# Down projection and attention output of a fused block as row-tiled units of 64 rows

## The chip, the cores and the metric

The kernel runs on one core of a Trainium2 chip. The metric is the device time of one execution in microseconds (us). Five engines run side by side, each through a queue of its own: TensorE (PE in the profile; its weight loads are listed apart as PEld), VectorE (DVE), ScalarE (ACT), GpSimd (POOL) and SyncE (SP), which here only starts DMAs. TensorE writes its sums to PSUM, which the kernel uses as eight banks of 128 partitions by 512 float32 numbers (the tile `ps_all`). ScalarE and VectorE read them from there.

## The reference

```python
x  = A_x                                  # (1, 2048, 576), bfloat16
xn = layernorm(x)
qkv = xn @ A_wqkv                         # 32 heads of 18
pq, pk = phi(q), phi(k)                   # phi(t) = (t + 1 if t > 0 else exp(t)) + 1e-6
kv, z = einsum(pk, v), sum(pk)            # per head: 18 x 18, and 18
o  = (pq @ kv) / (pq . z + 1e-6)
attention = o @ A_wo                      # 576 x 576
ffn = (gelu(xn @ B_w_gate) * (xn @ B_w_up)) @ B_w_down      # 576 -> 4608 -> 576
out = x + attention + ffn
```

## The kernel before, in words

**Tokens and stages.** The 2048 tokens are 16 tiles of 128 (`NS`); four tiles make a stage of 512 tokens (`sc`, `NSC` = 4, `TPC` = 4). The head of the kernel (until about 75.8 us) normalises x, transposes it into `xnT`, projects K for all tokens and Q for the first stage, runs the first 14 gate/up tiles (`RAW`), and builds the 32 products kv of all tokens as blocks on the diagonal of `kvT`. `kvT` holds five chunks of heads: four of 7 heads (126 rows) and one of 4 heads (72 rows).

**A stage.** The loop over `sc` (L955) does for each stage, in this order: the Q projection of the stage's four tiles (`late_q`, L855, from the second stage on; stage 0 has its Q from the head), gate/up (`gu_pair`, L804, 18 calls of two units each, of which stage 0 has the last 11), and the down part (L968 to 989). `hT` then holds gelu(gate) * up of the stage, 36 slices of 128 (`NF`).

**Two forms of matmul.** Gate/up and the Q projection contract over 576 = 4 x 128 + 64. They are built as `_Unit` (L242): the array is used as two row tiles, rows 0 to 63 (`LO`) and 64 to 127 (`HI`), which work side by side on different banks. In the first part (`p1`), LO adds to the unit's first bank and HI to its second, step by step. In the second part (`p2`) they change banks: LO adds to the second bank and HI to the first. In between, an empty instruction on GpSimd (`swap`, L263) waits for the last matmul of the first part, and the second part's first matmul on the second bank waits for it. The order in `gu_pair` and `late_q` puts another unit's part between the two parts of a unit. All these matmuls are issued at L253. The down part uses the whole array, 128 rows to one bank.

**The down part before.** A tile (`_DownTile`, L905) takes two banks, one for each half of the 576 output columns (288 and 288; the very last tile 448 and 128, `LAST_MID`). `down` (L929) issues for one half the 36 matmuls over `hT` and w_down (L935) and the 4 over the first four chunks of the attention (L940: `pqT`, the normalised and transposed Q features, against `m_sb`, the product kv x Wo). The fifth chunk has 64 rows and is kept twice, in LO and in HI; `pair` (L921) runs it for both halves side by side, as two half-array matmuls (L923). Tiles 0 and 1 of a stage run `pair` first; tiles 2 and 3 run it after all of the stage's `down` calls, or, in the last stage, before tile 2's. `add` (L945) lets VectorE add x to one half (L949); SyncE writes the tile out.

**kv x Wo.** `m_sb` is made once, in stage 0. The fifth chunk is made by `m_last_unit` (L880), a `_Unit` of one step in gate/up block `M_UNIT` = 10; ScalarE copies it to `m_last`, and SyncE's DMAs spread it in blocks 12 and 14. The other four are made by `m_product` (L870): two full-array matmuls each (L875) put between the down matmuls of tile 0's first half, at f = 8, 14, 20 and 26, with a copy by ScalarE after each.

**What sets the order.** From L704 on the program's order is the order of the instructions on each engine; nothing reorders them. Banks are handed out in pairs by a ring (`two_banks`, L126): four pairs, so a pair comes back after four grants, and its next user waits for its last reader. `load_late_wq` (L865) refills `wo2` with the Q weights once its Wo has been used. All weight loads and outputs stand in one queue, SyncE's.

```python
def p2(self):
    for kt in self.then:
        m = self.mm(1, LO, kt, False, kt == self.then[-1])
        if kt == self.then[0]:
            tc.add_manual_dep(m.ins, self.turn.ins.name, SYNC, ...)
        self.mm(0, HI, kt, False, kt == self.then[-1])
```

Of the kernel before, what the change touches and what calls it, by code (L numbers as in the profile page):

```python
# [14 lines left out]
P = 128  # L15
HP = 64
# [3 lines left out]
DH = 18  # L20
F = 4608
NS = S // P
NF = F // P
SC = 512
NSC = S // SC
TPC = SC // P
HALF = D // 2
KT = 5
HCH = [7, 7, 7, 7, 4]
HOFF = [0, 7, 14, 21, 28]  # L30
NCH = len(HCH)
# [58 lines left out]
def kernel(  # L90
# [11 lines left out]
    nc = tc.nc  # L102
# [14 lines left out]
    ps_all = psum.tile([P, 8, 512], F32, name="ps_all")  # L117
# [4 lines left out]
    LO, HI = slice(0, HP), slice(HP, P)  # L122
# [3 lines left out]
    def two_banks(ring=banks):  # L126
        return [ring.next(), ring.next()]
# [3 lines left out]
    kvT = persist.tile([P, NCH, CR], BF16, name="kvT")  # L131
# [8 lines left out]
    hT = h_store[:].rearrange("p (f t) -> p f t", t=SC)  # L140
# [137 lines left out]
    def gu_unit(blk, i, two, relay):  # L278
        wg, wu = gu_blocks[blk]
        wr = wr_pairs[blk // 2]  # L280
        c0 = (blk % 2) * GUB * P + i * P
        at = blk // NB * SC

        def lhs(a, rows, kt):
            if kt == 4:
                return wr[rows, c0:c0 + P]
            return (wg, wu)[a][rows, kt, i * P:(i + 1) * P]

        return _Unit(
            [ps_all[:, b, :] for b in two], lhs, lambda a, rows, kt: xnT[rows, kt, at:at + SC], relay,  # L290
        )
# [92 lines left out]
    for n in range(NS):  # L384
        first = 1.5 * n if n < 4 else 9.0 + 3.0 * (n - 4)
# [154 lines left out]
    for name in line:  # L540
# [3 lines left out]
        kind, n = name[0], int(name[1:].rstrip("ab"))  # L544
# [4 lines left out]
        if kind == "t":  # L549
            two = (tp_banks[n], tp_banks[n] + 1)  # L550
# [6 lines left out]
        if name[-1] == "b":  # L557
            u = pending[-1 if name[:2] == pending[-1].name else -2]
# [3 lines left out]
        u = _Chain()  # L562
        u.name, u.at = name[:2] if name[-1] == "a" else name, clock
        if kind in "KQ":
            u.body = _Token(kind, n, head_banks if u.name in HEAD_T else banks)
            b = u.body.banks
# [6 lines left out]
        else:  # L573
            u.body = _Raw(n)
            b = u.body.two
            blk = n // GUB
# [103 lines left out]
    def z_stage(two):  # L680
# [12 lines left out]
        out=bm3, in_=bm3, compare_op=ALU.is_ge, fill=0.0, base=0, pattern=[[-DH, 7], [0, DH]], channel_multiplier=1,  # L693
    )
    nc.gpsimd.affine_select(
        out=bm3, in_=bm3, compare_op=ALU.is_ge, fill=0.0, base=DH - 1, pattern=[[DH, 7], [0, DH]], channel_multiplier=-1,
# [40 lines left out]
    wo2 = late_pool.tile([P, NCH, D], BF16, name="wo2")  # L737
    m_sb = late_pool.tile([P, NCH, D], BF16, name="m_sb")
    m_last = late_pool.tile([P, D], BF16, name="m_last")
    pqT = late_pool.tile([P, NCH, S], BF16, name="pqT")  # L740
# [5 lines left out]
    def wd(f):  # L746
        return wd_a[:, f, :] if f < WD_A else wd_m[:, f - WD_A, :] if f < WD_B else wd_c[:, f - WD_B, :]

    def load_wo():
        nc.sync.dma_start(wo2[:CR, 0:4, :], A_wo[0:4 * CR, :].rearrange("(c p) j -> p c j", p=CR))  # L750
        nc.sync.dma_start(wo2[:D - 4 * CR, 4, :], A_wo[4 * CR:D, :])
# [46 lines left out]
    for n in range(NS):  # L798
        late = n % TPC > 0
        den_jobs += [(den_mul, n)] + late * [(den_transpose, n - 1)] + [(den_inv, n), (den_scale, n)]  # L800
        den_jobs += (n % TPC == TPC - 1) * [(den_transpose, n)]
    M_UNIT, M_TAILS, M_ROWS = RAW // GUB + 3, RAW // GUB + 5, RAW // GUB + 7

    def gu_pair(sc, k):  # L804
        blk = sc * NB + k
        units = []
        aside = m_last_unit() if blk == M_UNIT else None
        if aside:
            aside.p1()
        for i in range(GUB):  # L810
            b = two_banks()
            u = gu_unit(blk, i, b, nc.gpsimd)
            if blk > RAW // GUB:
                load_gu(blk + NWBUF - 1, i)
            u.p1()
            units.append((b, u))
        if sc == 0 and k == RAW // GUB:
            load_wo()
        elif wd_left:
            load_wd(*wd_left.pop(0))  # L820
        if aside:
            aside.p2()
            m_last_copy(aside)
        for i, (b, u) in enumerate(units):
            u.p2()
            gl = fwork.tile([P, SC], F32, name="gl")
            nc.scalar.activation(out=gl[:], in_=ps_all[:, b[0], :], func=ACT.Gelu_apprx_tanh)  # L827
            nc.vector.tensor_tensor(out=hT[:, GUB * k + i, :], in0=ps_all[:, b[1], :], in1=gl[:], op=ALU.mult)  # L828
            for _ in range(min(len(gelus), 2)):
                gelu_now(gelus.pop(0))  # L830
            if den_jobs and ((i == 1 and 0 < k < NB - 1) if sc else 8 < k < 17):
                job, n = den_jobs.pop(0)
                job(n)
# [31 lines left out]
    def load_late_wq():  # L865
        nc.sync.dma_start(wo2[:, 0:4, :], A_wqkv[0:512, 0:D].rearrange("(kt p) c -> p kt c", p=P))
        for rows in (LO, HI):
            nc.sync.dma_start(wo2[rows, 4, :], A_wqkv[512:576, 0:D])

    def m_product(c, bank):  # L870
        rows = DH * HCH[c]
        for hf in range(2):
            b = bank(hf)
            hs = slice(hf * HALF, (hf + 1) * HALF)
            nc.tensor.matmul(  # L875
                ps_all[:rows, b, :HALF], lhsT=kvT[:rows, c, :rows], rhs=wo2[:rows, c, hs], start=True, stop=True,
            )
            nc.scalar.copy(out=m_sb[:rows, c, hs], in_=ps_all[:rows, b, :HALF])

    def m_last_unit():  # L880
        rows4 = DH * HCH[4]
        two = two_banks()
        outs = [ps_all[:rows4, b, :HALF] for b in two]
        return _Unit(
            outs, lambda i, rows, kt: kvT[rows, 4, :rows4], lambda i, rows, kt: wo2[rows, 4, i * HALF:(i + 1) * HALF],
            nc.gpsimd, first=(0,), then=(0,),
        )

    def m_last_copy(u):
        for i in range(2):  # L890
            nc.scalar.copy(out=m_last[:DH * HCH[4], i * HALF:(i + 1) * HALF], in_=u.outs[i])
# [13 lines left out]
    class _DownTile:  # L905
# [4 lines left out]

        def __init__(self, n):
            self.n, self.ts = n, slice(n * P, (n + 1) * P)
            self.banks = two_banks()
            self.opened = False
            mid = LAST_MID if n == NS - 1 else HALF
            self.parts = [slice(0, mid), slice(mid, D)]

        def acc(self, hf):
            return ps_all[:, self.banks[hf], 0:self.parts[hf].stop - self.parts[hf].start]

        def pair(self):  # L921
            for hf, rows in ((0, LO), (1, HI)):
                nc.tensor.matmul(  # L923
                    self.acc(hf), lhsT=pqT[rows, 4, self.ts], rhs=m_sb[rows, 4, self.parts[hf]],
                    start=not self.opened, stop=self.opened, skip_group_check=True,
                )
            self.opened = True

        def down(self, hf, todo):  # L929
            paired = self.opened  # L930
            j = self.n % TPC
            for f in range(NF):
                if f in todo:
                    todo[f]()
                nc.tensor.matmul(  # L935
                    self.acc(hf), lhsT=hT[:, f, j * P:(j + 1) * P], rhs=wd(f)[:, self.parts[hf]],
                    start=(f == 0 and not paired), stop=False, skip_group_check=True,
                )
            for c in range(4):
                nc.tensor.matmul(  # L940
                    self.acc(hf), lhsT=pqT[:, c, self.ts], rhs=m_sb[:, c, self.parts[hf]],
                    start=False, stop=(paired and c == 3), skip_group_check=True,
                )

        def add(self, hf):  # L945
# [9 lines left out]
    for sc in range(NSC):  # L955
        if sc:
            late_q(sc)
            nc.scalar.preload_act_table_set("gelu_apprx_tanh_and_others")
        for k in range(0 if sc else RAW // GUB, NB):
            gu_pair(sc, k)  # L960
            if sc == 0 and k in m_last_steps:
                m_last_steps[k]()
        while wd_left:
            load_wd(*wd_left.pop(0))

        if sc < NSC - 1:
            nc.scalar.preload_act_table_set("natural_log_exp_and_others")
        tiles = [_DownTile(sc * TPC + j) for j in range(TPC)]  # L968
        tiles[0].pair()
        tiles[1].pair()  # L970
        spare = tiles[2].banks + tiles[3].banks
        hooks = {8 + 6 * c: (lambda c=c: m_product(c, lambda hf: spare[(2 * c + hf) % 4])) for c in range(4)} if sc == 0 else {}
        for j, t in enumerate(tiles):
            if j == 2 and sc == NSC - 1:
                tiles[2].pair()
                tiles[3].pair()
            closed = t.opened
            for hf in range(2):
                t.down(hf, hooks if j == hf == 0 else {})
                if closed:  # L980
                    t.add(hf)
            if sc == j == 0:
                load_late_wq()
        for t in tiles[2:]:
            if sc < NSC - 1:
                t.opened = True
                t.pair()
                for hf in range(2):
                    t.add(hf)


# [28 lines left out]
```

## Time and profile before

| what | value |
|---|---|
| median of three runs | 507.29 us (507.22 to 508.05) |
| the profiled execution | 507.53 us |
| its span, first to last instruction | 505.8 us |
| TensorE's mean granted clock | 0.999 |
| matmuls and weight loads | 4768 each |

The span is divided by the stages as follows, by the starts of matmuls:

| part | start, us | length, us |
|---|---|---|
| head and kv | 0 | 75.8 |
| gate/up, stage 0 (22 units) | 75.8 | 43.0 |
| down part, stage 0 | 118.8 | 40.9 |
| late Q and gate/up, stage 1 | 159.7 | 74.3 |
| down part, stage 1 | 234.0 | 39.9 |
| late Q and gate/up, stage 2 | 273.9 | 74.3 |
| down part, stage 2 | 348.2 | 39.9 |
| late Q and gate/up, stage 3 | 388.1 | 74.3 |
| down part, stage 3 | 462.5 | 40.5 to the end of the span |

How to read it: busy time tells how long an engine had work in flight, and matmuls overlap, so one lasts longer than the distance to the next. The pace of a stream is read from the time that a piece of the chain with a known number of matmuls takes, or from the starts of two matmuls. A wait that ends on an engine other than TensorE does not lengthen the kernel while TensorE's own stream has no hole.

### The profile page before, as it was taken

The page shows a single profiled execution, that of the slowest core. Times are in us where ns is not written, and L with a number is a line of the kernel's source. Part 1 is how long each engine was busy: PE and PEld are TensorE (multiplying, and loading weights), DVE is VectorE, ACT ScalarE, POOL GpSimd, SP SyncE. Part 2 cuts the span into 40 slices and gives each one's busy share as a digit, 9 for nine tenths or more (in the row PEclk, how much of TensorE's full clock was granted, in tenths as well). Part 3 has the DMA queues.
Part 4 walks back from the last instruction along what each step waited for, and adds up shares of the span by engine and source line. Part 5 has one row for each costly group of instructions (what it writes and reads, how often), then busy time and mean ns, then how long its engine had stood idle before and what let it go on. Part 6 is the DMA issues. An engine that isn't in the chain of part 4 may idle for free.

```text
span 505.8 us, 11210 instructions
## 1 busy us (share of the span) xinstructions
PE 501.7 (99%) x4768; PEld 304.8 (60%) x4768; DVE 230.8 (46%) x483; ACT 152.0 (30%) x265; POOL 10.4 (2%) x34
## 2 busy tenths in 40 slices
PE   9999999999999999999999999999999999999997
PEld 7666784446777444446777444445777444445774
DVE  5768996773002655553002665553002665553100
ACT  6778735325001422332001522332001432232000
POOL 3110100000000000000000000000000000000000
PEclk9999999999999999999999999999999999999999
DMA  9998917993201465553001455653001455640000
GB/s 230 269 217 170 304 45 207 282 252 80 71 13 54 119 166 172 158 150 106 12 13 42 129 156 170 169 151 108 13 12 32 140 150 167 173 104 14 13 13 23
DMA packets 114123, 61.59 MB, mean 122 GB/s; under 512 B 23954, under 2 KB 114010, under 8 KB 114074
## 3 DMA queue, kind: packets, MB, share of 16 engines
q1 hardware_dynamic: 113802, 60.54, 45.3%
q8 instruction: 37, 0.61, 0.5%
q0 software_dynamic: 128, 0.21, 0.1%
q10 hardware_dynamic: 144, 0.15, 0.1%
q14 instruction: 12, 0.10, 0.1%
HBM read 53.60 MB, written 2.36 MB: 111 GB/s over the span
## 4 chain that ended last, share of the span: by engine, by line
PE 99%; DVE 0%; issue 0%
PE ps_all L253 62%; PE ps_all L935 28%; PE ps_all L636 3%; PE ps_all L940 3%; PE ps_all L231 1%; PE ps_all L923 0%; PE ps_all L644 0%; PE ps_all L663 0%; PE ps_all L358 0%; PE ps_all L875 0%; PE ps_all L237 0%; DVE res L949 0%; PE ps_all L682 0%; DVE warm L210 0%; DVE eps_ln L222 0%
## 5 line engine op out<-in xcount | busy, mean ns | idle before, releaser
L253 PE MATMUL ps_all<-xnT,wg 64*128 64x512 bf16 x1152 | 273.8, 376 | 0.0
L253 PE MATMUL ps_all<-xnT,wu 64*128 64x512 bf16 x1152 | 273.1, 376 | 0.0
L253 PEld LDWEIGHTS <-wg 64*128 64x128 bf16 x1152 | 108.3, 94 | 66.7
L253 PEld LDWEIGHTS <-wu 64*128 64x128 bf16 x1152 | 108.3, 94 | 65.4
L828 DVE TENSOR_TENSOR hT<-ps_all,gl 128x512 bf16<-128x512 f32 x130 | 89.8, 691 | 104.2 <-ACT gl L827 104.1
L935 PEld LDWEIGHTS <-hT 128*128 128x128 bf16 x1152 | 110.8, 98 | 30.9 <-issue 1.3
L827 ACT ACTIVATE gl<-ps_all 128x512 f32<-128x512 f32 x130 | 77.6, 597 | 164.1 <-PE ps_all L253 163.7
L949 DVE TENSOR_TENSOR res<-ps_all,x_sb 128x288 bf16<-128x288 f32 (+2 forms) x32 | 13.8, 455 | 146.3 <-PE ps_all L940 88.1
L935 PE MATMUL ps_all<-wd_a,hT 128*128 128x288 bf16 (+2 forms) x512 | 68.3, 286 | 0.0
L253 PE MATMUL ps_all<-xnT,wr 64*128 64x512 bf16 x288 | 54.9, 376 | 0.0
L935 PE MATMUL ps_all<-hT 128*128 128x288 bf16 (+2 forms) x384 | 52.4, 286 | 0.0
L849 ACT ACTIVATE gl<-ps_all 128x288 f32<-128x288 f32 x24 | 9.2, 409 | 121.4 <-PE ps_all L253 119.3
L935 PE MATMUL ps_all<-wd_m,hT 128*128 128x288 bf16 (+2 forms) x256 | 36.8, 286 | 0.0
L253 PEld LDWEIGHTS <-xnT 64*128 64x128 bf16 x504 | 26.6, 94 | 6.6 <-ACT xnT L363 0.3
L253 PEld LDWEIGHTS <-wr 64*128 64x128 bf16 x288 | 14.3, 94 | 16.3
L940 PE MATMUL ps_all<-m_sb,pqT 128*128 128x288 bf16 (+2 forms) x128 | 20.9, 286 | 0.0
L253 PE MATMUL ps_all<-wqkv_sb,xnT 64*128 64x288 bf16 x256 | 19.7, 283 | 0.0
L636 PE MATMUL ps_all<-hT,xn 128*128 128x288 bf16 x128 | 16.0, 286 | 0.0
L486 ACT CAST hT<-ps_all 128x1024 bf16<-128x1024 f32 x14 | 14.1, 1010 | 4.9 <-PE ps_all L253 4.5
L636 PEld LDWEIGHTS <-xn 128*128 128x128 bf16 x128 | 12.4, 98 | 3.5 <-issue 0.5
L940 PEld LDWEIGHTS <-pqT 128*128 128x128 bf16 x128 | 12.4, 98 | 3.3
L253 PE MATMUL ps_all<-wo,xnT 64*128 64x288 bf16 x216 | 13.7, 283 | 0.0
(100 smaller groups left out, 245.4 us busy)
## 6 DMA issues: line engine op xcount, KB each, us to landing
wg<-in_B_w_gate_dram SPq DMA_DIRECT2D x72, 256.0 KB, 3.0
wu<-in_B_w_up_dram SPq DMA_DIRECT2D x72, 256.0 KB, 3.5
wd_a<-in_B_w_down_dram SPq DMA_DIRECT2D x4, 576.0 KB, 8.5
wr<-in_B_w_gate_dram SPq DMA_DIRECT2D x35, 64.0 KB, 3.1
wr<-in_B_w_up_dram SPq DMA_DIRECT2D x35, 64.0 KB, 2.9
out_dram<-res SPq DMA_DIRECT2D x15, 144.0 KB, 1.8
x_sb<-in_A_x_dram SPq DMA_DIRECT2D x6, 288.0 KB, 5.0
hT<-in_B_w_down_dram SPq DMA_DIRECT2D x4, 432.0 KB, 5.6
```

Of the source, the lines that this page charges most:

```text
L231: nc.tensor.matmul(ps_all[:, 7, 0:P], lhsT=warm[:], rhs=warm[:], start=True, stop=True)
L253: return nc.tensor.matmul(self.outs[i], lhsT=self.lhs(i, rows, kt), rhs=self.rhs(i, rows, kt), start=start, stop=stop, skip_group_check=True,)
L486: nc.scalar.copy(out=hT[:, self.f:self.f + NF + 1:NF, :], in_=ps_all[:, self.two[0]:self.two[0] + 2, :],)
L636: nc.tensor.matmul(ps_all[:, two[hf], :HALF], lhsT=xn[:, n, kt * P:(kt + 1) * P], rhs=pk[:, n, hf * HALF:(hf + 1) * HALF], start=(n == gra ...
L827: nc.scalar.activation(out=gl[:], in_=ps_all[:, b[0], :], func=ACT.Gelu_apprx_tanh)
L828: nc.vector.tensor_tensor(out=hT[:, GUB * k + i, :], in0=ps_all[:, b[1], :], in1=gl[:], op=ALU.mult)
L849: nc.scalar.activation(out=e[:, :HALF], in_=acc, func=ACT.Exp)
L935: nc.tensor.matmul(self.acc(hf), lhsT=hT[:, f, j * P:(j + 1) * P], rhs=wd(f)[:, self.parts[hf]], start=(f == 0 and not paired), stop=False ...
L940: nc.tensor.matmul(self.acc(hf), lhsT=pqT[:, c, self.ts], rhs=m_sb[:, c, self.parts[hf]], start=False, stop=(paired and c == 3), skip_grou ...
L949: nc.vector.tensor_tensor(out=self.res[:, hs], in0=self.acc(hf), in1=x_sb[:, self.n, hs], op=ALU.add)
```

## The change

- Tiles 0 to 14 run their whole down part as a `_Unit`: 1 + 36 + 4 steps in the first part (the fifth chunk first), 36 + 4 in the second, each step one matmul of 64 rows on LO and one on HI. The parts alternate: first part of tile j, then second part of tile j - 1 and its two adds; the last tile of a stage has its second part right after that of the tile before.
- The very last tile (15) stays in full-array matmuls with its 448 and 128 columns. Its `pair` is issued between the first part of tile 14 and the second part of tile 13, the rest of it after tile 14.
- The five kv x Wo products all run as `_Unit`s of one step in gate/up blocks 10 to 14, the fifth chunk first (`M_ORDER`). The chunks of 126 rows are cut into 64 and 62. ScalarE's copies follow the second part at once.
- `load_late_wq` is issued after the first stage's tile 0 is finished, which is now after two first parts and one second part.

In the changed file, the units' matmuls stay at L253; `pair` is at L936, `down` at L943 and L948, the adds at L957.

```diff
+    M_ORDER = (4, 0, 1, 2, 3)
...
-        aside = m_last_unit() if blk == M_UNIT else None
+        c = M_ORDER[blk - M_UNIT] if M_UNIT <= blk < M_UNIT + NCH else None
+        aside = None if c is None else m_unit(c)
...
             aside.p2()
-            m_last_copy(aside)
+            if c == 4:
+                m_last_copy(aside)
+            else:
+                m_copy(c, aside)
...
-    def m_product(c, bank):
+    def m_unit(c):
         rows = DH * HCH[c]
...
-            nc.tensor.matmul(
-                ps_all[:rows, b, :HALF], lhsT=kvT[:rows, c, :rows], rhs=wo2[:rows, c, hs], start=True, stop=True,
-            )
-            nc.scalar.copy(out=m_sb[:rows, c, hs], in_=ps_all[:rows, b, :HALF])
...
         two = two_banks()
+        half = (LO, HI if c == 4 else slice(HP, rows))
         return _Unit(
...
+            [ps_all[:rows, b, :HALF] for b in two], lambda i, part, kt: kvT[half[part is HI], c, :rows],
+            lambda i, part, kt: wo2[half[part is HI], c, i * HALF:(i + 1) * HALF], nc.gpsimd, first=(0,), then=(0,),
         )
...
+        def unit(self):
+            def lhs(i, rows, k):
+                if k < 0:
+                    return pqT[rows, 4, self.ts]
+                return hT[rows, k, self.cols] if k < NF else pqT[rows, k - NF, self.ts]
+
+            def rhs(i, rows, k):
+                if k < 0:
+                    return m_sb[rows, 4, self.parts[i]]
+                return wd(k)[rows, self.parts[i]] if k < NF else m_sb[rows, k - NF, self.parts[i]]
+
+            every = range(NF + 4)
+            return _Unit([self.acc(0), self.acc(1)], lhs, rhs, nc.gpsimd, first=(-1, *every), then=every)
...
-        tiles[0].pair()
-        tiles[1].pair()
-        spare = tiles[2].banks + tiles[3].banks
-        hooks = {8 + 6 * c: (lambda c=c: m_product(c, lambda hf: spare[(2 * c + hf) % 4])) for c in range(4)} if sc == 0 else {}
+        last = tiles.pop() if sc == NSC - 1 else None
+        held = []
         for j, t in enumerate(tiles):
-            if j == 2 and sc == NSC - 1:
-                tiles[2].pair()
-                tiles[3].pair()
-            closed = t.opened
-            for hf in range(2):
-                t.down(hf, hooks if j == hf == 0 else {})
-                if closed:
-                    t.add(hf)
-            if sc == j == 0:
-                load_late_wq()
-        for t in tiles[2:]:
-            if sc < NSC - 1:
-                t.opened = True
-                t.pair()
+            u = t.unit()
+            u.p1()
+            held.append((t, u))
+            if j == len(tiles) - 1 and last:
+                last.pair()
+            for t, u in held[:-1] if j < len(tiles) - 1 else held:
+                u.p2()
                 for hf in range(2):
                     t.add(hf)
+            held = held[-1:]
+            if sc == 0 and j == 1:
+                load_late_wq()
+        if last:
+            for hf in range(2):
+                last.down(hf)
+                last.add(hf)
```

## The prediction, on record before the changed kernel ran

> **What bounds the kernel now.** I read the page first (busy time by engine, the chain that ended last), then who waited for whom on TensorE (PE), then the chain in order of time, and last the matmuls and weight loads of one stretch.
>
> ```profile
> PE 501.7 (99%) x4768; PEld 304.8 (60%) x4768; DVE 230.8 (46%) x483; ACT 152.0 (30%) x265; POOL 10.4 (2%) x34
> PE 99%; DVE 0%; issue 0%
> ```
>
> The first line is the page's engine row, the second the page's chain by engine. The list of waits has one row for PE:
>
> ```profile
> PE ps_all L231 <- DVE eps_ln L222: 1.1, 1, 1.1
> ```
>
> That wait is at the very start. Nothing else makes PE wait, so the end is set by PE's matmuls one after another. A change pays only if PE needs less time for its stream, and costs only if PE needs more or is made to wait. So I look at pace and at the seams. In the chain in order of time (start, length, what; a piece runs from the end of the one before it) the stage of tiles 4 to 7 reads:
>
> ```profile
> 159.47 0.35 PE ps_all L923 x4
> 159.82 74.34 PE ps_all L253 x720
> 234.16 0.24 PE ps_all L923 x4
> 234.41 4.52 PE ps_all L935 x36
> 238.93 0.49 PE ps_all L940 x4
> 239.41 4.41 PE ps_all L935 x36
> ...
> 273.71 0.35 PE ps_all L923 x4
> ```
>
> See two things. (a) Steady pace: 36 full-array matmuls (128 rows, 288 columns) take 4.41 us, 122.5 ns each. (b) Seams: the same 36 take 4.52 right after 64-row work (L923 has 64 rows), and the four 64-row matmuls of L923 take 0.24 after 64-row work but 0.35 after full-array work. Each change of the array's form, in either direction, so costs 0.11 us. By the starts of single matmuls behind these rows it is 0.096 at the seam and 0.010 at the next start: **0.106 us**.
>
> **The change, part by part.**
>
> *Tiles 0 to 14 as row-tiled units.* Before, a tile is 2 x 40 full matmuls (36 of L935, 4 of L940, two halves) and one pair at L923: 80 x 122.5 + 122.5 = 9.92 us. After, it is 82 half-array matmuls in the first part and 80 in the second, all 64 rows by 288 columns. That form is in the trace: the late Q projection of a stage, 72 matmuls with 72 weight loads, alternating in the same way, with the same relay through GpSimd. Asked for that stretch and L253 alone, the trace gives (length, PE busy and count, weight loads busy and count, clock, DMA):
>
> ```profile
> 159.66:164.07 4.41, 4.41 (x72) 3.49 (x72) 1.00 0.43 125
> ```
>
> 72 half-array matmuls take the 4.41 us that 36 full ones take: 61.25 ns each, and two of them do the work of one full matmul. A tile after: 162 x 61.25 = 9.92 us. So **the pace gives nothing**: 15 tiles x (9.92 - 9.92) = 0. The rows are good to 0.005 us in 36 pairs, 0.14 ns a pair; over 15 x 81 = 1215 pairs that leaves +-0.17 us, the main term of the error.
>
> *The waits that it adds.* The second part of each tile waits for GpSimd's relay of its first part's end. Behind that wait PE's whole stream is queued. But another tile's part (about 4.9 us) stands between, as in the late Q projection another unit's 0.6 us does, and there the 61.25 ns already include four such waits. The one tile whose parts have least between them is the last of a stage: 40 pairs of the tile before, 4.9 us. Cost 0. The banks: a tile takes two of eight, as before; the next stage's fourth Q unit needs the last tile's banks some 2.8 us after its end (five parts of 0.49 to 0.61), and two adds of 0.46 free them.
>
> *Seams.* Before: into full-array work at the start of each of four stages, out of it at the end of three; in the last stage out and in once more for the pairs of tiles 14 and 15:
>
> ```profile
> 482.60 0.28 PE ps_all L923 x3
> 482.89 0.06 issue
> 482.95 4.58 PE ps_all L935 x36
> ```
>
> These 4.92 us are 36 x 0.1225 = 4.41, a pair of 0.12, a pair whose 448 columns take 0.19, and two seams. So nine seams in all. After: gate/up, down tiles and late Q are all of 64 rows, and only tile 15 is left in 128, with its pair issued among 64-row work: one seam. **Removed: 8 x 0.106 = 0.85 us.**
>
> *kv x Wo.* Four chunks leave the first down tile:
>
> ```profile
> 119.17 1.09 PE ps_all L935 x8
> 120.26 0.25 PE ps_all L875 x2
> ```
>
> Eight such matmuls; the first stage's down part is 0.99 us longer than the second's (starts of the first pair to the first late Q matmul, 40.895 against 39.904). They become four units of two pairs in gate/up blocks. The fifth chunk already runs so: its second pair starts at 89.72 and the next work at 89.84. So 8 x 0.1225 = 0.98 come back: gain 0.01. Their weight load is of 126 columns; at L875 it takes 0.136 us instead of 0.098. Here it lies under a 64 x 512 pair (0.216 us), so 0; without that cover it would be 4 x 0.04.
>
> The units also take bank pairs out of the ring of four in five blocks running instead of one, so that a gate/up unit's banks are wanted again after three grants of other units and not after whole blocks. In the block with the fifth chunk (ScalarE, then VectorE, from the timeline):
>
> ```profile
> 90.05 0.69 ACT L891 CAST m_last<-ps_all 72x288 bf16<-72x288 f32 x2 [1.80 <-DMA wd_m<-in_B_w_down_dram]
> 90.91 0.60 ACT L827 ACTIVATE gl<-ps_all 128x512 f32<-128x512 f32 x1 [0.17 <-PE ps_all L253]
> 91.54 0.69 DVE L828 TENSOR_TENSOR hT<-ps_all,gl 128x512 bf16<-128x512 f32 x1 [0.91 <-ACT gl L827]
> ```
>
> The first unit ends at about 90.88 and its banks are free at 92.23, 1.35 us later. The next wish for them comes after the second unit's last 4 pairs (0.86), a kv x Wo pair (0.12) and a first part of 5 pairs (1.08): 2.06 us later. Margin 0.7 us. The two copies (0.69) fit under a second part (0.86), as the 0.17 of idle time before the gelu shows. VectorE gets nothing new there; its longest run ahead of that multiply, reduce to reciprocal (1.3 us), ends 1.06 us before the multiply (98.25, 99.31). Cost 0; if the cover failed, see the rivals.
>
> *Moved DMAs.* The load of the Q weights into wo2 is issued after the second first-part and the first tile's output on SyncE's queue, about 134 instead of 131.1; it is used at 159.7. With it nothing but output writes is queued. Cost 0.
>
> **Sum.** -0.85 - 0.01 = -0.86 us, of the profiled execution's 507.53 (span 505.8 and 1.7 around it): 506.67, span 504.95. The median of the runs is 507.29, 0.24 below that execution; taken off there: **506.4**, -0.17%. About 0.2% (1.0 us) is what a measurement of this kernel can tell from no change, so this likeliest case is "within".
>
> **Rivals.**
>
> *PE is fed too slowly (slower).* The tiles hold 2430 matmuls instead of 1230, each with a weight load, for about 40 us at a stretch; late Q shows the pace for 4.4 us. If delivery of instructions or weights has a floor of d ns a matmul above 61.25, 2430 x (d - 61.25) is added; it turns the sign from d = 61.6. The upper end of d is the pace of gate/up itself, 107.9 (a pair every 0.2158 us), the lower end none. For it: no longer stretch exists. Against it, from the head:
>
> ```profile
> 9.59 0.29 PE ps_all L358 x20
> 9.88 2.82 PE ps_all L253 x46
> ```
>
> Twenty matmuls with twenty loads in 0.29 us, 15 ns each, though a queue may have held them; and from 9.6 to 17.1 PE starts 136 matmuls, 55 ns each, without a wait, too many to have been held. So d is most likely below 55. At d = 63, 3% over late Q, it would be +4.3 - 0.9: 510.7.
> The Trainium skill, "TensorE: Matmul & The Clock Gate", section "Wait — 56ns, not 53.3ns?", has such a floor: about 62 ns a matmul where the sequencer's microcode decodes. By it the sum would be an estimated 2430 x 0.75 = +1.8, so 508.3; the 15 ns above speak against it, and I leave it a chance of 0.03. Its section "Back-to-back issue gap" has about 81 ns for streams of load and matmul at 128 columns; by that the estimate is +48 us, and the 61.25 ns of late Q speak against it. Chance of this rival, with both: 0.08.
>
> *Banks late in the five blocks.* If a VectorE step (0.94 for the scale and copies) fell ahead of the first unit's multiply, 0.94 - 0.7 = 0.25 us, four times: 1.0 us, which eats the gain: 507.4. Chance 0.07.
>
> *The seam does not go away.* If the 0.106 is paid at each tile's first matmul or relay too, or was drain that shows elsewhere: 507.3. Against it: L923 after gate/up work costs its plain 0.24. Chance 0.08.
>
> *The pairs run a little faster than the rows can tell* (0.3 ns: another 0.36 us): 506.0. Chance 0.07.
>
> **Numbers.** Forecast -0.86 +-0.17: chance 0.70, of which 0.17 lies beyond -1.0. Faster 0.17 + 0.07 = 0.24; slower 0.08 and 0.02 each from the second and third rival, 0.12; within 0.64. The range 505.9 to 507.4 takes in the forecast and all rivals but the first.
>
> **What would show it.** The chain should run as one piece of L253 from about 75.8 to the last stage's tile 15, with no PE wait but the first. From one late Q projection to the next, 114.25 us (273.71 to 387.96) should become 114.04. The first stage's gate/up should be 0.98 longer, its down part 1.2 shorter. A new PE wait on VectorE between 91 and 110 would be the second rival; more than 61.3 ns a matmul in a down tile the first.

## The result, and the profile after

The changed kernel takes 506.78 us (median of 20 runs, 506.22 to 509.1) against 507.49 us of the kernel before (20 runs beside it, 507.09 to 508.9). The ratio is 0.9986, with a 95% interval of 0.998 to 0.9993: 0.71 us less, between 0.36 and 1.0. Forecast were 506.4 and -0.86. The profiled execution of the changed kernel took 506.81 us, with a span of 505.1.

The engine row and the chain by engine, from the page of the changed kernel:

```profile
PE 500.3 (99%) x5976; PEld 375.3 (74%) x5976; DVE 230.1 (46%) x483; ACT 152.1 (30%) x265; POOL 10.5 (2%) x34
PE 98%; DMA 1%; SPq 0%; DVE 0%; issue 0%
```

There are 1208 more matmuls and as many more weight loads, and PE is still the chain. The 1% of DMA is a load of weights in the head, the end of which PE waits for; the list of PE's waits has it with 0.6 us:

```profile
PE ps_all L231 <- DVE eps_ln L222: 1.1, 1, 1.1
PE ps_all L253 <- DMA wqkv_sb<-in_A_wqkv_dram: 0.6, 1, 0.6
```

The second wait lies before anything that the change touches: a load of the first weights that came later in this execution. After the head there is no wait. The chain in order of time (start, length, what):

```profile
75.98 406.16 PE ps_all L253 x4846
482.14 0.06 PE ps_all L936
482.19 9.89 PE ps_all L253 x160
492.09 6.92 PE ps_all L943 x36
```

Eight of the nine seams are gone: the stretch of 406 us is one piece of half-array matmuls. L936 is tile 15's pair, and L943 its full-array part, with the one seam that is left ahead of it. The same 36 matmuls of 448 columns took 6.81 us in the kernel before, where they followed other full-array matmuls; the 0.11 on top is the seam.

Where the time went, by the starts of single matmuls (from the first gate/up matmul after the head, then from one late Q projection to the next, then to the end of the span):

| part | before, us | after, us | difference | forecast |
|---|---|---|---|---|
| head | 75.775 | 75.911 | +0.136 | 0 |
| stage 0 | 83.885 | 83.660 | -0.225 | -0.22 |
| stage 1 | 114.244 | 114.030 | -0.214 | -0.21 |
| stage 2 | 114.243 | 114.029 | -0.214 | -0.21 |
| stage 3, to the end | 117.673 | 117.447 | -0.226 | -0.21 |
| sum (span) | 505.82 | 505.08 | -0.74 | -0.86 |

The four stages give 0.88 us; two of the eight seams that went lie in each. The head takes 0.14 back. It is the same code, and over the nine executions profiled in this study the first gate/up matmul starts anywhere from 75.44 to 76.13. The two executions with the tiles as before have 75.44 and 75.78, the seven with row-tiled tiles 75.64 to 76.13; whether the change has a part in that is not shown.

### The profile page after: what moved, and what is told of

Its sections match the earlier page's. It is cut to its first block, busy times and chain, and to the rows that moved or that the text cites. A ratio compares the mean times of both kernels' runs of the same rounds, so it can differ in the third digit from the quotient of the medians.

```text
span 505.1 us, 13641 instructions
## 1 busy us (share of the span) xinstructions
PE 500.3 (99%) x5976; PEld 375.3 (74%) x5976; DVE 230.1 (46%) x483; ACT 152.1 (30%) x265; POOL 10.5 (2%) x34
## 4 chain that ended last, share of the span: by engine, by line
PE 98%; DMA 1%; SPq 0%; DVE 0%; issue 0%
PE ps_all L253 92%; PE ps_all L636 3%; PE ps_all L943 2%; DMA wqkv_sb<-in_A_wqkv_dram 1%; PE ps_all L644 0%; PE ps_all L663 0%; PE ps_all L948 0%; PE ps_all L358 0%; SPq L170 0%; SPq L165 0%; DVE res L957 0%; PE ps_all L682 0%; PE ps_all L936 0%
## 5 line engine op out<-in xcount | busy, mean ns | idle before, releaser
L253 PE MATMUL ps_all<-xnT,wg 64*128 64x512 bf16 x1152 | 276.3, 376 | 0.0
L253 PE MATMUL ps_all<-xnT,wu 64*128 64x512 bf16 x1152 | 271.5, 376 | 0.0
L253 PEld LDWEIGHTS <-wg 64*128 64x128 bf16 x1152 | 108.3, 94 | 49.9
L253 PEld LDWEIGHTS <-wu 64*128 64x128 bf16 x1152 | 108.3, 94 | 48.3
L253 PEld LDWEIGHTS <-hT 64*128 64x128 bf16 x2160 | 132.6, 94 | 0.4
L957 DVE TENSOR_TENSOR res<-ps_all,x_sb 128x288 bf16<-128x288 f32 (+2 forms) x32 | 13.2, 452 | 143.1 <-PE ps_all L253 134.7
L253 PE MATMUL ps_all<-wd_a,hT 64*128 64x288 bf16 x960 | 64.9, 283 | 0.0
L253 PE MATMUL ps_all<-xnT,wr 64*128 64x512 bf16 x288 | 59.0, 376 | 0.0
L253 PE MATMUL ps_all<-hT 64*128 64x288 bf16 x720 | 50.2, 283 | 0.0
L253 PE MATMUL ps_all<-wd_m,hT 64*128 64x288 bf16 x480 | 35.5, 283 | 0.0
L253 PEld LDWEIGHTS <-xnT 64*128 64x128 bf16 x504 | 29.2, 94 | 4.0 <-ACT xnT L363 0.3
L253 PEld LDWEIGHTS <-wr 64*128 64x128 bf16 x288 | 18.4, 94 | 12.1
L253 PE MATMUL ps_all<-m_sb,pqT 64*128 64x288 bf16 x270 | 23.4, 283 | 0.0
L253 PE MATMUL ps_all<-wqkv_sb,xnT 64*128 64x288 bf16 x256 | 19.7, 283 | 0.0
L253 PEld LDWEIGHTS <-pqT 64*128 64x128 bf16 x270 | 17.0, 94 | 0.3
L253 PE MATMUL ps_all<-wo,xnT 64*128 64x288 bf16 x216 | 13.8, 283 | 0.0
```

The lines of the kernel that those rows point to most:

```text
L253: return nc.tensor.matmul(self.outs[i], lhsT=self.lhs(i, rows, kt), rhs=self.rhs(i, rows, kt), start=start, stop=stop, skip_group_check=True,)
L957: nc.vector.tensor_tensor(out=self.res[:, hs], in0=self.acc(hf), in1=x_sb[:, self.n, hs], op=ALU.add)
```

## The experiments

My theory was: the gain is eight changes of the array's form at 0.106 us each. The pace, the move of kv x Wo and the new waits count for nothing. Rivals: a change of form costs nothing by itself and the gain comes from the move of kv x Wo; PE cannot be fed at twice the number of matmuls; the ring of banks is near a stall. In the ratios "before" is the kernel before, run beside the experiments: 507.53 us (21 runs) for the first four, 507.67 us (15 runs) for the last three. In the code, `u.rows` issues the pairs of a first part for the steps that it is given, and `u.swap` the empty instruction on GpSimd behind them.

**Sixty changes of form there and back, and the control.**

```diff
-            u.p1()
+            steps_ = (-1, *range(NF + 4))
+            for s0, s1 in ((0, 11), (11, 21), (21, 31), (31, 41)):
+                u.rows(steps_[s0:s1])
+                nc.tensor.matmul(t.acc(0)[:, 0:P], lhsT=warm[:], rhs=wd(0)[:, 0:P], start=False, stop=False, ...)
+            u.swap()
```

> The changed kernel, with 60 full-array matmuls put into the first parts of tiles 0 to 14 (four in each, weights all zero, 128 columns), so that the stream goes into full-array form and back 60 times more. My theory: each change of form costs 0.106 us, so 120 x 0.106 = 12.7 us, and the matmuls themselves 60 x 0.056 = 3.4 us: 506.8 + 16.1 = 522.9. Rival (a change of form costs nothing in the middle of a stream; the gain came from elsewhere): 3.4 us alone, 510.2.

The control puts two half-array matmuls at the same places, `warm[LO, :]` on the first bank and `warm[HI, :]` on the second.

> The control to the run before: the same work at the same 60 places, but as pairs of half-array matmuls (64 rows, zero weights, 128 columns, one on each bank), so no change of form. My theory and the rival both: 60 x 0.056 = 3.4 us, 510.2. The difference of the two runs, divided by 120, is the price of one change of form: 0.106 us by my theory, 0 by the rival.

| run | median, us | ratio to before (95%) |
|---|---|---|
| full-array, 120 changes of form | 522.97 | 1.0300 (1.0284 to 1.0316) |
| control | 510.19 | 1.0052 (1.0038 to 1.0065) |

The difference is 12.78 us; divided by 120 it is **0.1065 us a change of form**. The chain of the first of the two, in a first part of stage 0:

```profile
121.64 0.16 PE ps_all L984
121.81 1.33 PE ps_all L253 x20
123.14 0.16 PE ps_all L984
```

The same 20 half-array matmuls in the chain of the control, twice, with an added pair between them:

```profile
121.49 1.23 PE ps_all L253 x20
122.77 1.23 PE ps_all L253 x20
```

L984 is the full-array matmul of 128 columns: 0.16, where the control's pair in its place is worth 0.056, so about 0.11 on the way in. The 20 half-array matmuls after it take 1.33 where the control has 1.23: about 0.10 on the way back. From the first late Q projection to the second the two traces differ by 3.40 us, in which lie 32 changes of form: again 0.106 each. The price holds in the middle of a stream, in both directions, and the rival that it costs nothing there falls.

What the price is made of, no run tests by itself, but the traces point to a weight load that is not hidden. In the steady full-array stream of the kernel before, a load starts 0.12 us ahead of its matmul, beside the matmul before it (at L940, 487.25 and 487.37). Behind a seam it starts only 0.01 us ahead, after PEld has been idle; the first matmul of L935 starts at 482.95:

```profile
482.94 4.28 PEld L935 LDWEIGHTS <-hT 128*128 128x128 bf16 x36 [0.30 <-issue]
```

A load takes 0.094 to 0.098 us, near the 0.106 of a seam, and a seam with a longer load was dearer by about the difference (0.04, in the next experiment).

**The move of kv x Wo alone, and its undoing alone.** The first is the kernel before with `m_unit` and `M_ORDER` of the change and `hooks = {}`, tiles as before:

> The kernel before with one part of the change alone: kv x Wo as units in gate/up blocks 10 to 14, the down tiles in full-array form as before. My theory: all nine changes of form stay, so 507.5 as before (-0.01). Rival (the gain comes from moving kv x Wo): 506.8.

The second is the changed kernel with only the fifth chunk in gate/up, and the four products as full-array matmuls in the first part of tile 0:

```diff
-            u.p1()
+            if sc == j == 0:
+                steps_ = (-1, *range(NF + 4))
+                u.rows(steps_[:15])
+                spare = tiles[1].banks + tiles[2].banks + tiles[3].banks
+                for c in range(4):
+                    m_product(c, spare)
+                u.rows(steps_[15:])
+                u.swap()
+            else:
+                u.p1()
```

> The changed kernel with one part undone: the four kv x Wo products of 126 rows are full-array matmuls again, all eight in one place of the first tile's first part in stage 0. My theory: two changes of form more, 0.21 us, and nothing else: 507.0; the trace shows stage 0 from gate/up to the next Q projection 0.2 us longer. Rival (the gain comes from moving kv x Wo into gate/up): all of it is lost, 507.5.

| run | median, us | ratio to before (95%) |
|---|---|---|
| kv x Wo as units, tiles as before | 507.40 | 1.0000 (0.9991 to 1.0008) |
| tiles as units, kv x Wo in full-array form | 506.97 | 0.9988 (0.9979 to 0.9997) |

Against 507.53 of before, the move alone gives nothing that can be told from zero (its interval reaches less than 0.5 us either way, and the rival's 0.7 lies outside it), and the tiles alone give 0.56 (0.15 to 1.07). In the trace of the move alone stage 0 takes 83.91 us against 83.89 before, and the seams stand as before:

```profile
119.86 4.52 PE ps_all L934 x36
...
159.16 0.35 PE ps_all L922 x4
```

4.52 and 0.35 are the seams of before, at L934 and L922 here. In the other trace stage 0 is 0.46 us longer than in the changed kernel, not 0.21: two seams (0.21); 0.04 at the first seam, where the loads are of 126 columns and take 0.132 to 0.136 us instead of 0.094 to 0.098; and 0.22 at the last two of the eight products, where six banks were too few and PE waited for ScalarE's copies. That last part is of my arrangement. The time, 506.97 against 506.78, cannot tell 0.21 from 0.46; the trace can.

**How fast PE can be fed.**

```diff
-            u.p1()
+            u.rows()
+            for r in range(160):
+                for hf, rows in ((0, LO), (1, HI)):
+                    u.last = nc.tensor.matmul(
+                        t.acc(hf)[:, 0:P], lhsT=hT[rows, r % NF, t.cols], rhs=warm[rows, :],
+                        start=False, stop=False, ...)
+            u.swap()
```

> The changed kernel with 160 more pairs of half-array matmuls in each of tiles 0 to 14 (weights from hT, each with its own weight load, moving data all zero, 128 columns): a stream that asks for a matmul and a weight load every 28 ns, 9 us at a stretch. It asks how far PE can be fed. My theory (no floor above 28 ns a matmul): 15 x 160 x 0.056 = 134 us more, 641. Rival (a floor of 55 ns a matmul, the fastest long stretch of the trace before): 15 x 320 x 0.055 = 264, 771. By the floor of about 62 ns in the Trainium skill, TensorE: Matmul & The Clock Gate, section Wait - 56ns, not 53.3ns?, an estimate of 298 more, 804.

640.82 us, ratio 1.2622 (1.2599 to 1.2645). The chain of this kernel in stage 0:

```profile
138.87 8.93 PE ps_all L984 x320
147.80 9.92 PE ps_all L253 x162
```

L984 is the added stream: 320 matmuls, each with a load of its own, in 8.93 us, 27.9 ns each, and it ran so 15 times. The 162 of L253 beside it are one first and one second part of a tile, at 61.2 ns each. So no floor above 28 ns shows for this form, and the changed kernel's tiles ask for less than half of the matmuls per time that PE was fed here.

**A tighter ring of banks.**

```diff
         if aside:
             aside.p1()
+            if c < 4:
+                two_banks()
```

> The changed kernel, where blocks 11 to 14 of gate/up each take one more pair of banks out of the ring and leave it unused. My theory: a unit's banks are free 1.35 us after its end, and are now wanted 0.98 us after it instead of 2.06, so PE waits about 0.37 us in each of four or five blocks, in all 1.5 to 1.9 us: 508.5, with PE waiting for VectorE or ScalarE between 91 and 110 us. Rival (the ring has slack to spare; the margin of 0.7 us is wrong): 506.8 and no wait.

510.53 us, ratio 1.0057 (1.0043 to 1.0071): 2.9 us above the kernel before that ran beside it, where the changed kernel was 0.7 below the one beside it, so about 3.6 us for the grants, twice what I expected. Waits of PE, and a part of the chain of this kernel:

```profile
PE ps_all L253 <- DVE hT L835: 2.3, 6, 0.5
```

```profile
91.79 0.69 DVE hT L835
92.48 0.74 DVE pn L783 x2
...
93.64 0.61 DVE hT L835
94.25 0.04 issue
94.29 2.24 PE ps_all L253 x17
```

The kind of stall is as expected: PE takes up its stream when the multiply (hT, L835) is through. The first one, read from starts of matmuls, costs 0.38 us against 0.37 expected. But I had counted the first units of a block alone. The second units are wanted early here too, and in every other block the scale and its two copies (L783, L789, L792) stand before their multiply: their stalls are 0.65 us, twice. By the starts of matmuls there are six large holes of 0.38, 0.66, 0.51, 0.59, 0.65 and 0.59 us and three small ones of 0.06 to 0.08, together 3.6, the whole of the loss. (The list of waits has 2.3 for the large ones, since it counts from the end of the matmul before, and a matmul is recorded with 0.28 to 0.38 us where the pace is 0.12 to 0.22.) So the ring does bind, with one grant more per block. In the changed kernel the multiply that frees the first unit's banks ran as the margin had it:

```profile
91.05 0.60 ACT L832 ACTIVATE gl<-ps_all 128x512 f32<-128x512 f32 x1 [0.17 <-PE ps_all L253]
91.68 0.69 DVE L833 TENSOR_TENSOR hT<-ps_all,gl 128x512 bf16<-128x512 f32 x1 [0.91 <-ACT gl L832]
```

The banks were free at 92.37 and wanted at 92.91: 0.54 us to spare, not 0.7. I had measured the wish from the time at which the unit's last sums are written, when it runs from the time at which the next matmul can start, 0.16 earlier.

**Tile 15 as a unit too.**

```diff
-    LAST_MID = 448
+    LAST_MID = HALF
-        last = tiles.pop() if sc == NSC - 1 else None
+        last = None
```

> The changed kernel with tile 15 as a unit too, halves of 288 and 288 columns. My theory: the last change of form goes (-0.11 us) and the uneven pair of 448 and 128 columns becomes an even one (-0.07), but both halves now end together, so two adds of about 0.45 us follow the last matmul instead of one of 0.29, and the last output is larger: about +0.6. Sum +0.4: 507.2. Rival (the form alone matters): 506.6.

507.46 us, ratio 0.9997 (0.9988 to 1.0006), where the changed kernel had 0.9986; the two intervals overlap, so the traces have to tell them apart. The last lines of the two timelines, this kernel first:

```profile
501.63 0.82 DVE L957 TENSOR_TENSOR res<-ps_all,x_sb 128x288 bf16<-128x288 f32 x2 [4.08 <-PE ps_all L253]
502.12 0.81 SPq L959 DMA_DIRECT2D out_dram<-res  x2
```

```profile
502.03 0.29 DVE L957 TENSOR_TENSOR res<-ps_all,x_sb 128x128 bf16<-128x128 f32 x1 [1.61 <-PE ps_all L948]
502.35 0.33 SPq L959 DMA_DIRECT2D out_dram<-res  x1
```

PE's last matmul ends 0.13 us earlier after the start of the last late Q (forecast 0.18), but two adds of 0.82 in place of one of 0.29, and two output issues after them, make the time from PE's last matmul to the end 3.87 us instead of 3.08; the eight other traces have 3.08 to 3.10. The sign was as forecast; the end was under-estimated, by 0.2. Tile 15 as a unit does not pay: the seam that is left costs 0.11, and what it buys is worth 0.8.

## Why the prediction was right

- *PE's stream is the bound, and pays only by pace and seams.* Held: after the head PE has no wait in the changed kernel, and each difference behind the head is a term of PE's stream.
- *Seams, -0.85.* Held: 0.1065 us each by the pair of runs, and in the trace the stages are 0.88 shorter together with the 0.01 of kv x Wo.
- *Pace 0, with +-0.17 us.* Held: 162 half-array matmuls take 9.92 us. The error allowed for was not used; the stages came out within 0.02 us.
- *Waits and banks 0.* Held, with a cover that the ring experiment shows to be needed: one grant more per block costs 3.6 us. My step had looked at the first units alone, its margin of 0.7 was 0.54, and the rival's 0.94 for the scale and its copies was too small: in the trace of before they hold VectorE for 1.15 us (92.15 to 93.30). In the changed kernel the second units' banks go to a kv x Wo unit a whole block later, so it did no harm here.
- *kv x Wo -0.01.* Held: the move alone changed nothing that can be measured. From the first gate/up matmul to the first of the down part stage 0 grew by 0.98 us, and from there to the first late Q matmul it shrank by 1.205 (40.895 to 39.690); forecast were 0.98 and 1.2.
- *Moved DMAs 0.* Held, though the load of the Q weights was issued at 136.3 and not at about 134: it is used at 159.6, and PE waits for nothing there.
- *PE fed too slowly, chance 0.08.* Refuted in the form that it was put: 27.9 ns a matmul with a load each. By the Trainium skill's figure of about 62 ns ("TensorE: Matmul & The Clock Gate", "Wait — 56ns, not 53.3ns?") the feed experiment would have taken an estimated 160 us more, and the changed kernel itself 2. The measurement decides: there is no such floor here. The section ties it to a mode of decoding, and no run here shows which mode is set. The Trainium skill's 81 ns of "Back-to-back issue gap" (same page) are not seen in this form either.
- *The time.* Forecast 506.4, measured 506.78: the stages gave what was forecast. In the profiled executions the head took 0.14 back, and the span came out 0.13 above its forecast. Of the 0.35 us in the medians, 0.20 is the median of before, 507.29 in the three runs that the sum was set against and 507.49 in the twenty; the other 0.15 lies within the interval of the measurement. The range of 505.9 to 507.4 takes in almost no change at all, so that the time lay in it says little: the table of the stages and the price of 0.1065 us bear the mechanism out.

What stays open: why the head's start of gate/up scatters by 0.7 us between executions. It was not tried; its DMA waits differ from one trace to the next. Open too is what a change of form is made of: the weight load that is not hidden fits its size, but was not tested alone.

## What to carry to other kernels

When PE's stream has no holes, count its seams: find in the chain a piece of known length that follows work of another form, take the difference, multiply. Two row tiles at equal columns neither gained nor lost pace here (61.25 ns a matmul against 122.5 for the full array), so they can be used to keep neighbouring work in one form. Before taking more grants from a ring of buffers, work out the time to the next wish for each user between two grants, not for the first alone.

## What the runs showed of the hardware that was not expected

The two row tiles can drift apart and stay apart at no cost. In the changed kernel the two matmuls of a pair start 0.003 us apart up to the first kv x Wo unit of 126 columns, whose weight loads take 0.133 us instead of 0.094. The four such units bring it to 0.038 us, and it stays so through the stages, until tile 15's uneven pair makes it 0.027. It costs nothing that shows: stages 1 and 2 take 114.03 us with it, and 114.03 in the experiment with the products back in full-array form, where it is 0.003. From the timeline of the changed kernel, ahead of the first such unit and after the second:

```profile
91.49 0.38 PE L253 MATMUL ps_all<-xnT,wu 64*128 64x512 bf16 x1
91.49 0.38 PE L253 MATMUL ps_all<-xnT,wg 64*128 64x512 bf16 x1
...
98.45 0.38 PE L253 MATMUL ps_all<-xnT,wu 64*128 64x512 bf16 x1
98.48 0.37 PE L253 MATMUL ps_all<-xnT,wg 64*128 64x512 bf16 x1
```

Each row tile keeps its own pace, 0.216 us here and 0.1225 us in the down tiles. In the experiment with the products back in full-array form the offset is 0.003 through the stages up to tile 15's pair, and with kv x Wo alone moved it is 0.038 in stage 0 and back at 0.003 after the first stage's full-array tiles. So it comes from those units and not from the tiles, and a change of form takes it away. The unit of 72 columns (loads of 0.110 us) left it at 0.003; the later four differ from it in their slower loads, and in HI's 62 rows beside LO's 64. Which of the two does it was not tested.

The time in which a weight load was under way rose from 60% to 74% of the span while the span fell. That comes from the offset and not from the row tiles: the experiment with the products back in full-array form has the same row-tiled tiles without the offset, and the share of before.

```profile
PE 500.5 (99%) x5968; PEld 304.9 (60%) x5968; DVE 230.1 (46%) x483; ACT 151.8 (30%) x265; POOL 10.5 (2%) x34
```

With a pair 0.003 us apart its two loads run at the same time and count once; 0.038 us apart they count longer, for the same work at the same pace. So here that share does not say how near to its bound PE is.
